# A decayed-attention, gated-product and slot-mixture kernel: the first sixteen items fetched further ahead, into six buffers

## The chip, the cores and the metric

The kernel runs on one core of one Trainium2 chip. The metric is the device time of one execution in microseconds (us), as a median of several runs. In a profile the engines are PE (TensorE: matmuls; PEld is its weight load), DVE (VectorE), ACT (ScalarE), POOL (GpSimd) and SP (SyncE, which here does nothing but issue transfers, in the order of its queue). "Span" is the time from the first to the last instruction.

## The reference, cut to what matters

```python
def _attn_ref(q, k, v, s):                      # B, H, S, D = 4, 8, 576, 64
    scores = scale * np.matmul(q, k.transpose(0, 1, 3, 2))
    cum = np.cumsum(np.maximum(s, 0.0), axis=-1)
    bias = -(cum[:, :, :, None] - cum[:, :, None, :])
    scores = np.where(causal, -1000000000.0, scores + np.minimum(bias, 0.0))
    attn = softmax(scores)                      # written out with max, exp, sum
    return np.matmul(attn, v)
...
def _moe_ref(x, w1, w2, w3, w_out):             # x: 2304 x 512
    a = x @ w1
    b = x @ w2
    return (a * b @ w3) @ w_out
...
def _moe2_ref(x, phi, w1, w2):                  # 8 experts, 4 slots each
    logits = x @ phi
    ...                                         # softmax over tokens, two expert layers, softmax over slots
    return c @ slot_out
```

All arrays are float32; the four matrices of `_moe_ref` arrive as 64-bit words (float64) and are converted on the chip.

## The kernel before, in words

Attention is cut into 40 items. Items 0 to 7 are heads 0 to 7 with the query tiles 0, 1, 2; items 8 to 15 are the same heads with the tiles 3, 4; items 16 to 39 are one head each with all five tiles. The first 16 items (`NF32`) multiply in float32: the item's tile `raw` holds queries and keys in 64 partitions, and four more partitions (64 to 67) get the decay rows of its head, so that one matmul gives score and decay. Items from 16 on are split into a rounded part `qa` and a rest `qb` by DVE and POOL.

An item passes through these steps. `att_fetch` issues the transfers of queries and keys; `att_prep` issues those of the decay rows and, for every second head, of the values `v` of two heads, and from item 16 on computes `qa` and `qb`. `att_scores` multiplies on PE (L334), adds the mask and takes the row minimum on DVE (L337) into the score buffer `sc`, and takes the exponential on ACT (L342). `att_norm` adds and inverts the row sums on DVE (L351, L352) and scales on POOL (L355). `att_transpose` turns the scores on PE (L370, and L384 for the diagonal blocks), into two PSUM buffers that ACT copies out (L372, L386). `att_pv` multiplies by the values of two heads (PE L110) and writes `x` (ACT L419, DVE L420). Then come the gated products `gl` (L432), which need `x` of four pairs of heads.

Beside this, the words of the matrices are fetched 512 KB at a time into three buffers (`fetch_words`, L178) and converted: ACT L186, DVE L189, L190, L193, then ACT L217 and POOL L218 for `w12`; ACT L186, L197, DVE L198, L201 for the others.

Buffers of a tile tag are a ring: the third `raw` waits until the first is read out. Before, `raw` has two buffers (`NRW`), `sc` three (`SCB`), and `qa` and `qb`, first used by item 16, two each (`QAB`). The program calls the steps in an order that `att_steps` and `weave` write out. SP's queue keeps that program order; the instructions on PE, DVE, ACT and POOL are put in order by the scheduler of the framework, so that a change of buffers or of waits also reorders those queues.

The lines around the fetch, as they stand before:

```python
            prep = [(0, lambda n=n: att_prep(n + 1, ap))] if n + 1 < N else []
            if n + 2 < N:
                prep += [(0, lambda n=n: att_fetch(n + 2, ap))]
```

Of the kernel before, what the change touches and what calls it, by code (L numbers as in the profile page):

```python
# [10 lines left out]
F32 = mybir.dt.float32  # L11
# [10 lines left out]
P = 128  # L22
B, H, S, D = 4, 8, 576, 64
# [24 lines left out]
def attn_glu_softmoe_kernel(  # L48
# [14 lines left out]
    nc = tc.nc  # L63
# [19 lines left out]

    NW, NRAW, NG4, NX, NE_ = 8, 3, 4, 6, 11
    NRW, SCB, PTB, QAB, VB = 2, 3, 2, 2, 2
    NF32, NDIR, ND = 16, 2, 1

    A1, CA, CB1, CB, GB1, GB, GC = 0.6, 8, 16, 26, 8, 16, 24

# [174 lines left out]
    hd = {}  # L264
    ITEMS = [(h, t) for t in ((0, 1, 2), (3, 4)) for h in range(H)] + [(h, (0, 1, 2, 3, 4)) for h in range(H, NH)]

    def att_fetch(n, ap):
        h, tiles = ITEMS[n]
        if h % 2 == 0:
            b, c = divmod(h // 2, H // 2)  # L270
            for blk, (_, nt, own) in enumerate(BLK):
                if own[0] in tiles:
                    x_t[b, blk, c] = xpl.tile([P, 2, nt], F32R, tag=f"x{blk}", name=f"x_{b}_{blk}_{c}", bufs=NX)
        q0, q1 = QT[tiles[0]][0], sum(QT[tiles[-1]])
        raw = ap.tile([P, 2, S], F32, tag="raw", name=f"raw_{n}", bufs=NRW)
        m = 64 if n < NF32 else P
        if q0:
            nc.sync.dma_start(raw[:m, 0, q0:q1], qk[h, 0, :m, q0:q1])
            nc.sync.dma_start(raw[:m, 1, :q1], qk[h, 1, :m, :q1])
        else:  # L280
            nc.sync.dma_start(raw[:m, :, :q1], qk[h, :, :m, :q1].rearrange("n p t -> p n t"))
        hd[n] = dict(raw=raw, q0=q0, q1=q1)

    def att_prep(n, ap):
        h, tiles = ITEMS[n]
        t = hd[n]
        raw, q0, q1 = t["raw"], t["q0"], t["q1"]
        if h % 2:
            vt = ap.tile([P, 9, 2, D], F32, tag="v", name=f"v_{n}", bufs=VB)
            nv = 2 * tiles[-1] + 1  # L290
            nc.sync.dma_start(vt[:, :nv], v[h // 2, :, :nv])
            t["v"] = hd[n - 1]["v"] = vt
        if n < NF32:
            rows = raw
        else:
# [22 lines left out]
    def att_scores(n, i, ap):  # L318
        t, tiles = hd[n], ITEMS[n][1]
        if i == tiles[0]:  # L320
            t["nmax"] = sm.tile([P, 6], F32, tag="nmax", name=f"nmax_{n}")
            t["rsum"] = rsum_t[n % 3]
            t["sc"] = ap.tile([P, 1600], F32, tag="sc", name=f"sc_{n}", bufs=SCB)
        nmax, rsum, mul = t["nmax"], t["rsum"], t["mul"]
        q0, r = QT[i]
        W = q0 + r
# [304 lines left out]
    def att_steps(ap):  # L631

        groups = [[] for _ in range(B + 1)]
        N = len(ITEMS)
        for n in range(N + 1):
            tiles = ITEMS[n][1] if n < N else ()
            old = [i for i in ITEMS[n - 1][1] if i] if 0 < n <= N else []
            sc = [(0.2 + 0.3 * i, lambda i=i, n=n: att_scores(n, i, ap)) for i in tiles]
            tr = [(0.2 + 0.3 * i, lambda i=i, n=n: att_transpose(n - 1, i, ap)) for i in old]
            norm = [(0, lambda n=n: att_norm(n - 1))] if 0 < n <= N else []  # L640
            prep = [(0, lambda n=n: att_prep(n + 1, ap))] if n + 1 < N else []
            if n + 2 < N:
                prep += [(0, lambda n=n: att_fetch(n + 2, ap))]
            blks = [k for k in range(2) if BLK[k][2][0] in ITEMS[n - 1][1]]
            pv = [(1.4, lambda n=n, k=k: att_pv(n - 2, k)) for k in blks] if n > 0 and n % 2 == 0 else []
            groups[min(B, max(0, (n - 1) // H))] += [
                *sc[:1], *norm, *sc[1:2], *prep, *sc[2:3], *tr[:1], *sc[3:4], *tr[1:2], *sc[4:], *tr[2:], *pv
            ]
        return groups
# [78 lines left out]
    with tc.tile_pool(name="att", bufs=1) as ap:  # L728
# [15 lines left out]
        hd["ap"] = ap  # L744
        att = att_steps(ap)
        decay_rows()
        att_prep(0, ap)
        for k in range(2, NRAW):
            fetch_words(k, ap)
        decay_store()  # L750

        def masks():

# [348 lines left out]
```

## Time and profile before

| | |
|---|---|
| median of 3 runs | 574.28 us (573.58 to 574.37) |
| span of the profiled execution | 569.3 us (4.98 below the median; the time of that execution itself is not listed apart) |
| PE busy | 519.9 us, 91% of the span |
| DVE, ACT, POOL busy | 316.7, 311.6, 194.7 us |
| transfers | 118.04 MB, 207 GB/s on average |

PE is busy almost everywhere except in the first tenth of the span and at its very end. A stretch in which PE is idle or runs at a lower clock is therefore where time can be found, and the other engines matter as far as PE waits for them.

### The profile page before, as it was taken

The page shows a single profiled execution, that of the slowest core. Times are in us where ns is not written, and L with a number is a line of the kernel's source. Part 1 is how long each engine was busy: PE and PEld are TensorE (multiplying, and loading weights), DVE is VectorE, ACT ScalarE, POOL GpSimd, SP SyncE. Part 2 cuts the span into 40 slices and gives each one's busy share as a digit, 9 for nine tenths or more (in the row PEclk, how much of TensorE's full clock was granted, in tenths as well). Part 3 has the DMA queues.
Part 4 walks back from the last instruction along what each step waited for, and adds up shares of the span by engine and source line. Part 5 has one row for each costly group of instructions (what it writes and reads, how often), then busy time and mean ns, then how long its engine had stood idle before and what let it go on. Part 6 is the DMA issues. An engine that isn't in the chain of part 4 may idle for free.

```text
span 569.3 us, 11835 instructions
## 1 busy us (share of the span) xinstructions
PE 519.9 (91%) x4288; PEld 434.2 (76%) x4288; DVE 316.7 (56%) x966; ACT 311.6 (55%) x845; POOL 194.7 (34%) x247
## 2 busy tenths in 40 slices
PE   1886999788899999999899999999999999999993
PEld 1664788666788897989899879898888999853452
DVE  6558676769987376656565757456640311243333
ACT  4577667666876665845576667456833321321222
POOL 5447531526678456252255444333210000000000
PEclk9998999979999999999999999999999999999997
DMA  6557557657763353536556554465351996689976
GB/s 197 188 164 229 183 180 252 238 170 237 224 218 116 119 165 108 169 95 205 176 155 189 170 185 139 156 200 163 123 212 48 368 411 233 238 295 423 421 296 235
DMA packets 38810, 118.04 MB, mean 207 GB/s; under 512 B 4224, under 2 KB 10560, under 8 KB 35296
## 3 DMA queue, kind: packets, MB, share of 16 engines
q1 hardware_dynamic: 36832, 113.74, 57.9%
q10 hardware_dynamic: 1920, 3.54, 2.5%
q8 instruction: 34, 0.56, 0.4%
q14 instruction: 24, 0.20, 0.1%
HBM read 102.11 MB, written 11.60 MB: 200 GB/s over the span
## 4 chain that ended last, share of the span: by engine, by line
PE 38%; DMA 5%; DVE 4%; ACT 2%; issue 1%; POOL 0%; SPq 0%; DVEq 0%; POOLq 0%; ACTq 0%
PE gl L432 17%; DMA raw_w<-in_w 4%; PE x_ps L110 3%; PE o_ps L1003 3%; PE h_ps L965 3%; PE gn_ps L602 2%; PE sc_ps L334 2%; PE pt_ps L370 2%; PE z_ps L110 1%; DVE w_w L198 1%; PE ptd_ps L384 1%; PE y_ps L889 1%; PE lg L110 1%; DVE sc L337 1%; DVE w_w L201 1%
## 5 line engine op out<-in xcount | busy, mean ns | idle before, releaser
L432 PE MATMUL gl<-x,w12t 128*128 128x320 f32 (+1 forms) x1536 | 241.0, 307 | 4.2 <-DVE nmax L337 2.4
L432 PEld LDWEIGHTS gl<-x,w12t 128*128 128x128 f32 x1536 | 215.4, 194 | 12.8 <-DVE nmax L337 4.3
L342 ACT ACTIVATE sc<-sc,nmax 128x64 f32<-128x64 f32 (+4 forms) x160 | 89.8, 563 | 40.4 <-DVE nmax L337 38.7
L355 POOL TENSOR_SCALAR sc<-sc,rinv 128x64 f32<-128x64 f32 (+4 forms) x160 | 91.0, 585 | 56.7 <-DVE rinv L352 45.8
L313 POOL TENSOR_TENSOR qa<-raw,qa 64x576 fp32r<-64x576 f32 x24 | 36.9, 1536 | 145.5 <-DVE qa L307 134.0
L337 DVE CUSTOM_DVE_ANT_0 sc<-sc_ps,mask 128x64 f32<-128x64 f32 (+4 forms) x160 | 65.3, 424 | 35.6 <-PE sc_ps L334 32.8
L372 ACT COPY pt<-pt_ps 128x128 f32<-128x128 f32 (+3 forms) x128 | 52.4, 422 | 27.8 <-PE pt_ps L370 18.1
L370 PE MATMUL pt_ps<-ident,sc 128*128 128x128 f32 x320 | 56.6, 288 | 5.4 <-POOL sc L355 4.3
L370 PEld LDWEIGHTS pt_ps<-ident,sc 128*128 128x128 f32 x320 | 39.5, 146 | 16.7 <-POOL sc L355 7.7
L334 PE MATMUL sc_ps<-qa 128*128 128x64 f32 (+1 forms) x144 | 46.2, 334 | 5.3 <-DVE nmax L337 2.3
L334 PE MATMUL sc_ps<-raw 68*128 68x288 f32 (+4 forms) x96 | 33.8, 495 | 17.8 <-DMA raw<-rows 13.3
L438 ACT COPY a<-gl 128x256 f32<-128x256 f32 (+1 forms) x64 | 25.4, 397 | 38.4 <-PE gl L432 34.8
L110 PE MATMUL x_ps<-pt,v 128*64 128x256 f32 (+1 forms) x384 | 45.8, 352 | 0.0
L334 PE MATMUL sc_ps<-qb 68*128 68x64 f32 (+1 forms) x144 | 43.7, 307 | 0.7 <-issue 0.7
L310 POOL TENSOR_TENSOR qb<-raw,qa 64x576 fp32r<-64x576 f32 x24 | 38.0, 1582 | 2.2 <-issue 0.5
L974 POOL MEMSET ht<- 128x1024 f32 x2 | 1.9, 954 | 107.3 <-DVE ew L878 98.4
L334 PEld LDWEIGHTS sc_ps<-raw 68*128 68x128 f32 x96 | 19.5, 241 | 23.4 <-issue 12.4
L110 PEld LDWEIGHTS x_ps<-pt,v 128*64 128x64 f32 x384 | 31.1, 139 | 6.9 <-issue 0.9
L186 ACT ACTIVATE w_w<-raw_w 128x512 f32<-128x512 f32 x32 | 21.6, 674 | 23.5 <-DMA raw_w<-in_w 22.4
L420 DVE TENSOR_TENSOR x<-x_ps,x 128x320 fp32r<-128x320 f32 (+1 forms) x32 | 14.0, 453 | 36.5 <-ACT x L419 36.5
L334 PEld LDWEIGHTS sc_ps<-qa 128*128 128x128 f32 x144 | 27.5, 191 | 8.7 <-DVE nmax L337 4.1
L605 ACT COPY gn<-gn_ps 128x512 f32<-128x512 f32 x40 | 22.7, 582 | 15.2 <-PE gn_ps L602 14.8
(180 smaller groups left out, 786.5 us busy)
## 6 DMA issues: line engine op xcount, KB each, us to landing
ew<-in_ew SPq DMA_DIRECT2D x27, 1024.0 KB
raw_w<-in_w SPq DMA_DIRECT2D x32, 512.0 KB
raw<-in_qk SPq DMA_DIRECT2D x24, 576.0 KB
v<-in_v SPq DMA_DIRECT2D x16, 576.0 KB
raw_w3t<-in_w3t SPq DMA_DIRECT2D x16, 512.0 KB
raw_wot<-in_wot SPq DMA_DIRECT2D x8, 512.0 KB
raw_wo<-in_wo SPq DMA_DIRECT2D x8, 512.0 KB
w_d<-w_w SPq DMA_DIRECT2D x8, 512.0 KB
```

The source lines that it names most:

```text
L110: mm = nc.tensor.matmul(out_, lhs, rhs, start=start, stop=stop)
L310: nc.gpsimd.tensor_tensor(out=qb[0:64, 1, :q1], in0=rk[0:64, :q1], in1=qa[0:64, 1, :q1].bitcast(F32), op=ALU.subtract)
L313: nc.gpsimd.tensor_tensor(out=qa[64:, 0, q0:q1], in0=rq[64:, q0:q1], in1=qa[64:, 0, q0:q1].bitcast(F32), op=ALU.subtract)
L334: nc.tensor.matmul(pp[:r, : z - a], x[:, 0, q0 : q0 + r], x[:, 1, a:z], start=x is mul[0], stop=x is mul[-1])
L337: nc.vector.tensor_tensor_reduce(out=sc[:r, a:z], in0=pp[:r, : z - a], in1=hd["mask"][:r, m0 : m0 + z - a], scale=-0.125, scalar=3.0e38 if ...
L342: nc.scalar.activation(out=sc[:r, :W], in_=sc[:r, :W], func=AF.Exp, bias=nmax[:r, i : i + 1], scale=-1.0, accum_out=rsum[:r, i, 0:1],)
L355: nc.gpsimd.tensor_scalar(out=sc, in0=sc, scalar1=rinv[:, i : i + 1], scalar2=1.0, op0=ALU.mult, op1=ALU.mult)
L370: nc.tensor.transpose(tp[:, j * P : (j + 1) * P], sc[:, j * P : (j + 1) * P], ident)
L372: t["turned", i] = nc.scalar.copy(out=pt[:, p0 : p0 + step * (i - 1) + 1 : step], in_=tp[:, : i * P].rearrange("p (j q) -> p j q", q=P))
L432: nc.tensor.matmul(acc[:, :nt], w12_t[fc][:, wi, n, kc], x_t[b, blk, kc][:, xi], start=k == 0, stop=k == 3 * KC - 1)
L438: nc.scalar.copy(out=a_sb[:, :nt], in_=acc[:, :nt])
L605: st["turned", blk, k, h] = nc.scalar.copy(out=gn[:r, 4 * h : 4 * h + 4].rearrange("p c f -> p (c f)"), in_=tp[:r])
```

## The change

Four things are done. The fetch of queries and keys of an item below 16 is issued four items ahead (before: two), and that of its decay rows three ahead (before: one). The tiles of these items use the tags `raw`, `qa` and `qb` in turn, two buffers each, six in all. The transfer of the values gets its own function and stays one item ahead. Of the items 0 to 7, an odd one uses the upper half of the score buffer of the even one before it. At the start, the decay rows of items 0 and 1 and the fetches of items 2 and 3 are issued before the loop, item 2's fetch ahead of the third block of words.

```diff
-    NF32, NDIR, ND = 16, 2, 1
+    NF32, NDIR, ND, FAR = 16, 2, 1, 3
...
-        raw = ap.tile([P, 2, S], F32, tag="raw", name=f"raw_{n}", bufs=NRW)
+        tag = ("raw", "qa", "qb")[n % 3] if n < NF32 else "raw"
+        raw = ap.tile([P, 2, S], F32, tag=tag, name=f"raw_{n}", bufs=NRW)
...
+    def att_values(n, ap):
+        h, tiles = ITEMS[n]
+        if h % 2:
+            vt = ap.tile([P, 9, 2, D], F32, tag="v", name=f"v_{n}", bufs=VB)
+            nv = 2 * tiles[-1] + 1
+            nc.sync.dma_start(vt[:, :nv], v[h // 2, :, :nv])
+            hd[n]["v"] = hd[n - 1]["v"] = vt
+
...
-            t["sc"] = ap.tile([P, 1600], F32, tag="sc", name=f"sc_{n}", bufs=SCB)
+            if n >= H or n % 2 == 0:
+                t["sc"] = ap.tile([P, 1600], F32, tag="sc", name=f"sc_{n}", bufs=SCB)
+            else:
+                t["sc"] = hd[n - 1]["sc"][:, 800:]
...
-            prep = [(0, lambda n=n: att_prep(n + 1, ap))] if n + 1 < N else []
-            if n + 2 < N:
-                prep += [(0, lambda n=n: att_fetch(n + 2, ap))]
+            prep = [(0, lambda n=n: att_values(n + 1, ap))] if n + 1 < N else []
+            d = FAR if n + FAR < NF32 else 1 if NF32 <= n + 1 < N else 0
+            if d:
+                prep += [(0, lambda m=n + d: att_prep(m, ap))]
+            d = FAR + 1 if n + FAR + 1 < NF32 else 2 if NF32 <= n + 2 < N else 0
+            if d:
+                prep += [(0, lambda m=n + d: att_fetch(m, ap))]
...
-        att_prep(0, ap)
+        for n in range(NDIR):
+            att_prep(n, ap)
+        att_fetch(2, ap)
         for k in range(2, NRAW):
             fetch_words(k, ap)
         decay_store()
+        for n in range(NDIR, FAR):
+            att_fetch(n + 1, ap)
+            att_prep(n, ap)
```

The change moves instructions on every engine. Three places show it. The number behind a tile's name is its item (or matrix block) and then a running number.

On SP near the start, before the change, from the third block of words (`raw_w12_1_0`) to the decay rows of item 2:

```order
L178 DMA raw_w12_1_0_153<-in_w12 128x512
L166 DMA rows_d_101<-rows_0_130 32x4x512
L166 DMA rows_d_101<-rows_1_131 32x4x512
L167 DMA rows_d_101<-rows_2_132 256x1x64
L291 DMA v_1_168<-in_v 128x640
L300 DMA raw_1_116<-rows_0_130 2x2x320
L300 DMA raw_1_116<-rows_1_131 2x2x320
L281 DMA raw_2_173<-in_qk 64x2x320
L178 DMA raw_w12_1_1_203<-in_w12 128x512
L302 DMA raw_2_173<-rows_d_101 4x2x320
```

The same place on SP after the change, from the second of item 1's two decay-row transfers to the fourth block of words:

```order
L304 DMA raw_1_116<-rows_1_131 2x2x320
L282 DMA raw_2_156<-in_qk 64x2x320
L178 DMA raw_w12_1_0_158<-in_w12 128x512
L166 DMA rows_d_101<-rows_0_130 32x4x512
L166 DMA rows_d_101<-rows_1_131 32x4x512
L167 DMA rows_d_101<-rows_2_132 256x1x64
L282 DMA raw_3_163<-in_qk 64x2x320
L306 DMA raw_2_156<-rows_d_101 4x2x320
L290 DMA v_1_176<-in_v 128x640
L306 DMA raw_3_163<-rows_d_101 4x2x320
L282 DMA raw_4_180<-in_qk 64x2x320
L178 DMA raw_w12_1_1_209<-in_w12 128x512
```

The decay rows of item 1 and the queries and keys of item 2 now stand ahead of the third block of words, and those of items 3 and 4 ahead of the fourth.

On PE around the transposes of item 0, before the change (`pt_ps` and `ptd_ps` are the two PSUM buffers in turn):

```order
L370 MATMUL pt_ps_0_1_214<-ident_86,sc_0_159 128x128
L370 MATMUL pt_ps_0_2_217<-ident_86,sc_0_159 128x128 x2
L334 MATMUL sc_ps_2_0_0_228<-raw_2_173 128x64
L334 MATMUL sc_ps_2_1_0_238<-raw_2_173 128x192
L334 MATMUL sc_ps_2_2_0_248<-raw_2_173 128x320
L384 MATMUL ptd_ps_0_221<-ident_86,sc_0_159 128x128 x3
```

The same place on PE after the change:

```order
L377 MATMUL pt_ps_0_1_220<-ident_86,sc_0_167 128x128
L377 MATMUL pt_ps_0_2_223<-ident_86,sc_0_167 128x128 x2
L391 MATMUL ptd_ps_0_227<-ident_86,sc_0_167 128x128 x3
L341 MATMUL sc_ps_2_0_0_234<-raw_2_156 128x64
L341 MATMUL sc_ps_2_1_0_244<-raw_2_156 128x192
L341 MATMUL sc_ps_2_2_0_254<-raw_2_156 128x320
```

The diagonal transposes of item 0 moved from behind item 2's scores to ahead of them.

On POOL around the split of item 16, before the change (L355 scales the scores of an item, L313 and L310 make the rests of `qa` and `qb`):

```order
L355 TENSOR_SCALAR sc_13_989<-sc_13_989,rinv_13_1057 128x576
L313 TENSOR_TENSOR qa_16_1238<-raw_16_1096,qa_16_1238 64x576
L310 TENSOR_TENSOR qb_16_1237<-raw_16_1096,qa_16_1238 64x576
L355 TENSOR_SCALAR sc_14_1052<-sc_14_1052,rinv_14_1196 128x448
L355 TENSOR_SCALAR sc_14_1052<-sc_14_1052,rinv_14_1196 128x576
```

The same place on POOL after the change:

```order
L362 TENSOR_SCALAR sc_13_965<-sc_13_965,rinv_13_1054 128x576
L362 TENSOR_SCALAR sc_14_1049<-sc_14_1049,rinv_14_1192 128x448
L362 TENSOR_SCALAR sc_14_1049<-sc_14_1049,rinv_14_1192 128x576
L317 TENSOR_TENSOR qa_16_1205<-raw_16_1092,qa_16_1205 64x576
L314 TENSOR_TENSOR qb_16_1204<-raw_16_1092,qa_16_1205 64x576
```

The scaling of item 14 moved ahead of the split of item 16; on DVE the reciprocal of item 14 likewise stands ahead of item 16's casts now. Elsewhere the scores of items 5 to 9 stand earlier on PE among the other work, and on DVE the write of `x` for the fourth pair of heads (L420) stands behind the conversion of block `w12_5_0`, where before it stood behind that of `w12_6_0`. Whole groups change places up to about item 18 and single instructions up to item 22; from there on the queues of PE, DVE, ACT and POOL are the same as before.

## Rows read from the trace of the kernel before

**Rows 1.** The page: busy us, share of the span and instructions of each engine.

```profile
PE 519.9 (91%) x4288; PEld 434.2 (76%) x4288; DVE 316.7 (56%) x966; ACT 311.6 (55%) x845; POOL 194.7 (34%) x247
```

**Rows 2.** Windows: length, busy us of PE, PEld, DVE, ACT, POOL, PEclk, DMA share, GB/s.

```profile
9.00:37.00 28.00, 21.44 (x82) 15.75 (x82) 16.44 (x62) 17.71 (x56) 14.30 (x21) 1.00 0.57 175
37.00:64.00 27.00, 21.01 (x138) 15.80 (x138) 21.51 (x60) 18.89 (x53) 16.16 (x19) 0.87 0.65 202
64.00:100.00 36.00, 34.99 (x238) 28.60 (x238) 23.35 (x63) 24.33 (x58) 10.70 (x13) 1.00 0.69 224
100.00:125.00 25.00, 19.03 (x127) 15.44 (x126) 17.61 (x40) 14.99 (x37) 10.65 (x8) 0.86 0.64 211
```

**Rows 3.** Waits of PE, 9 to 126 us: total, times, longest.

```profile
PE sc_ps L334 <- DMA raw<-rows: 13.3, 2, 9.6
...
PE sc_ps L334 <- DMA raw<-rows_d: 3.2, 4, 1.5
```

**Rows 4.** Timeline of PE, scores: start, us, and idle time before.

```profile
15.79 2.47 PE L334 MATMUL sc_ps<-raw 68*128 68x64 f32 x6 [3.71 <-DMA raw<-rows]
...
18.69 2.36 PE L334 MATMUL sc_ps<-raw 68*128 68x64 f32 x6
...
35.58 1.33 PE L334 MATMUL sc_ps<-raw 68*128 68x64 f32 x6 [0.43 <-issue]
```

**Rows 5.** Windows of 2 us (columns as in the windows above).

```profile
50.00:52.00 2.00, 0.33 (x1) 0.14 (x1) 1.97 (x5) 1.70 (x5) 2.00 (x4) 0.90 1.01 245
52.00:54.00 2.00, 1.17 (x2) 0.79 (x3) 1.92 (x4) 0.12 (x1) 1.29 (x1) 0.50 1.05 298
...
56.00:58.00 2.00, 2.00 (x10) 1.81 (x8) 2.00 (x7) 1.60 (x4) 0.71 (x1) 0.50 0.05 8
```

**Rows 6.** Timeline of SP near the start (the DMA queue's issues).

```profile
8.40 0.39 SPq L178 DMA_DIRECT2D raw_w<-in_w  x1
...
12.09 1.32 SPq L300 DMA_DIRECT2D raw<-rows  x2
13.51 0.69 SPq L281 DMA_DIRECT2D raw<-in_qk  x1
...
32.44 0.33 SPq L291 DMA_DIRECT2D v<-in_v  x1
```

**Rows 7.** Waits of SP, 9 to 60 us.

```profile
SPq L291 <- PE x_ps L110: 6.5, 2, 6.2
```

**Rows 8.** Timeline of DVE and ACT.

```profile
12.67 0.67 ACT L186 ACTIVATE w_w<-raw_w 128x512 f32<-128x512 f32 x1 [0.72 <-DMA raw_w<-in_w]
...
21.77 0.56 ACT L342 ACTIVATE sc<-sc,nmax 128x320 f32<-128x320 f32 x1
...
29.33 0.23 DVE L337 CUSTOM_DVE_ANT_0 sc<-sc_ps,mask 128x64 f32<-128x64 f32 x1 [0.99 <-PE ptd_ps L384]
...
30.86 0.55 ACT L342 ACTIVATE sc<-sc,nmax 128x320 f32<-128x320 f32 x1
...
38.96 0.43 ACT L419 CAST x<-x_ps 128x320 fp32r<-128x320 f32 x1
```

**Rows 9.** Groups of instructions by line, 9 to 56 us: busy us, mean ns of one.

```profile
L342 ACT ACTIVATE sc<-sc,nmax 128x64 f32<-128x64 f32 (+4 forms) x27 | 13.0, 480 | 4.0 <-DVE nmax L337 3.0 <-POOL sc L355 0.8
...
L193 DVE SCALAR_TENSOR_TENSOR w_w<-raw_w,w_w 128x512 uint32<-128x512 uint32 x10 | 8.5, 851 | 0.0
L190 DVE SCALAR_TENSOR_TENSOR w_w<-raw_w,w_w 128x512 int32<-128x512 int32 x9 | 6.4, 709 | 0.1
```

**Rows 10.** Timeline: the fourth `x`, and the split of item 16 on DVE, POOL and PE.

```profile
67.11 0.49 DVE L420 TENSOR_TENSOR x<-x_ps,x 128x320 fp32r<-128x320 f32 x1 [0.95 <-ACT x L419]
...
99.86 0.46 DVE L307 CAST qa<-raw 128x576 fp32r<-128x576 f32 x1 [1.89 <-DMA raw<-in_qk]
...
103.42 2.76 POOL L355 TENSOR_SCALAR sc<-sc,rinv 128x448 f32<-128x448 f32 x2
...
104.56 0.55 PE L370 MATMUL pt_ps<-ident,sc 128*128 128x128 f32 x3 [1.94 <-POOL sc L355]
```

More of the change, by code (lines that the diff above doesn't have):

```diff
@@ L287, in att_prep @@
         raw, q0, q1 = t["raw"], t["q0"], t["q1"]
[L288 to L292, printed above, removed]
         if n < NF32:
```

## The prediction

> **What bounds the kernel now.** I read the page first: PE is busy for 91% of the span [rows 1], so only stretches where it waits or runs slowly can give time back. The windows then show where these are. From 64 to 100 us PE is busy 34.99 of 36 us; from 9 to 37 it lacks 6.6 us, from 37 to 64 it lacks 6.0, from 100 to 125 again 6.0 [rows 2]. The change moves whole groups in the queues up to about item 18, whose work lies around the end of these windows, and single instructions up to item 22, so these three gaps are what it can reach. What is won there should reach the end whole: the later queues are as before, and the engines in them wait for each other, so that a shift is passed on. I count the single swaps behind item 18 at nothing, with a bound of 1 us to either side, about what one such order cost DVE at 29.33 (0.99) [rows 8].
>
> Next I read who ends PE's waits. Scores waited for decay rows 13.3 us in two waits, of which 9.6 are the start itself; that leaves 3.7. For decay rows out of memory they waited 3.2 us in four waits [rows 3]. So transfers hold PE for 6.9 us. Second comes the clock. Six score matmuls take 2.47 us at 15.79 and 1.33 at 35.58 [rows 4], and after a stretch in which PE was busy 0.33 of 2 us the granted clock is 0.50, the lower level of 1.2 GHz; it is still there at 56 to 58 with PE fully busy [rows 5]. A late transfer thus costs more than its wait. Third come the engines behind PE: from 37 to 64 us DVE is busy 21.51 of 27 us and ACT 18.89 [rows 2], so there they are nearly as full as PE, and a score that is computed earlier still has to pass them.
>
> **The change, step by step.** *The start gives little.* Item 1's scores stood idle for 3.71 us before 15.79 [rows 4]; their rows are now issued right behind item 0's, so they can start at 12.1. But the third block of words now stands on SP behind those rows (1.32) and item 2's queries (0.69), so it goes out at 10.4 and not at 8.40 [rows 6]. Before, ACT took it up at 12.67 after a wait for exactly this transfer [rows 8], which is 4.3 us after issue; now that makes 14.7. On ACT and DVE its conversion stands between the second and the third tile of item 1, and both engines keep their order. So: 14.7, ACT 0.67, a first DVE step and the third tile's minimum (about 0.5 each), its exponential about 0.75, which gives 17.1; then ACT's copies of item 0's transposes, whose PSUM the diagonal transposes need, and these now stand ahead of item 2's scores. That puts item 2's scores at about 18.4, and they were at 18.69 [rows 4]. The fourth block of words moves back likewise, behind items 3 and 4, by about 2.3 us, and stands on ACT ahead of item 2's last exponential: I get 21.9 for that, and it was 21.77 [rows 8]. Up to here I count **0 us**; the bounds are a loss of 1 (the words land later still) and a gain of 3.7 (the words land early enough).
>
> *Items 4 to 7.* Before, DVE stood 0.99 us at 29.33 for the score buffer, until item 1's diagonal transposes were done, and item 4's last exponential came at 30.86 [rows 8]. With two items in a buffer this wait is gone, and the rows of items 3 and 4 are there. PE goes through item 3, item 1's transposes and item 4 without a stop from 20.8 to 26.7, at the slow rate of rows 4, and the last exponential comes at about 28.3: 2.5 us earlier. After that items 5, 6 and 7 follow before the second pair's `x`, which comes at about 41.8 by the same reckoning, where it was 38.96 [rows 8]: 2.85 later, but with two more items through their exponentials. Two items are six exponentials of 0.48 us [rows 9] plus their read-outs, about 3.4 us of ACT. ACT works at 18.89 of 27 [rows 2], so this is 4.8 us of the time before; net 2.0. By DVE, at 21.51 of 27, the two items are worth some 3.2 us; net 0.4. Taken between: **1.2 us**.
>
> *From the second to the fourth `x`.* Up to the fourth `x` DVE now converts two and a half blocks fewer. A block costs DVE 0.85 and 0.71 [rows 9] and a third step of about 0.5, so 2.1 us, and 5.2 for them all. In the stretch before, DVE was full (1.97 and 1.92 of 2) just while PE stood nearly idle [rows 5], so a part of this comes off the path: at DVE's rate of 0.80 up to 6.5 us, at worst nothing, if PE's own work fills the place. The half clock from about 52 to 59 is worth another 3.5 us (seven busy us at half rate), but it lies in the same place and I don't count it twice. I take half of the 6.5, **3.2 us**, because PE, which was full at half clock from 54 on, becomes the next to be late. So the fourth `x`, at 67.11 before [rows 10], comes at about 62.7. The conversions left over fall into the stretch to 100 us, in which DVE idles 12.65 of 36 us while PE idles 1 [rows 2]: they cost nothing there. If that cover were gone, they would cost their 5.2 us.
>
> *Item 16.* Before, DVE stood 1.89 us for item 16's queries; POOL split item 16 first and scaled item 14 only at 103.42, and PE waited 1.94 us for that [rows 10]. Now the scaling comes first on POOL and its reciprocal first on DVE, and the fetch of item 16 waits for item 12's buffer and not for item 14's. I count the **1.9 us** of PE. The split is then later by the 2.76 us of that scaling at most; POOL was free from 106 to 112, so this is hidden. Bounds: 0 (another wait takes its place) and 4 (the clock of 0.86 in this stretch [rows 2] improves too).
>
> *The values and the copies.* The transfers are as many as before and of the same size. Splitting the values from the rows and the new tags cost no instruction. The wait of SP that remains is that for the values of items 4 and 5, which need the product of the first pair: 6.2 us until 32.44 before [rows 6, 7]. Queued behind it are now item 7's rows, item 8's queries and the seventh block of words, where before it was item 5's rows. I get that product's end at about 33.5 and item 7's rows 2.5 us later, just when PE comes to them: 0, bounds 0 and minus 2.
>
> Sum: 0 + 1.2 + 3.2 + 1.9 = 6.3 us. The span of 569.3 becomes 563.0. The profiled execution's own time isn't listed; the median lies 4.98 above the span, and with the same distance the time is **568.0 us**.
>
> **A rule weighed.** At 52 to 54 us the DMA share is 1.05 [rows 5], and there lies PE's longest wait for rows out of memory, 1.5 us [rows 3], before item 9. The Trainium skill, "DMA: Bandwidth & Descriptors", section "Issuing engines are not separate DMA queues", says that all transfers run on the same 16 DMA engines and interleave; by that rule an earlier fetch makes bytes no fewer, and what is pulled ahead pushes the words back. This trace agrees in that place, and for the whole stretch (share 0.65, rows 2) it leaves room. By the row for the stretch the sum stays; by the rule applied to the burst alone, the wait at item 9 stays and the sum is 3.4 lower. That is the third rival.
>
> **The rivals.** *All waits go.* If the words land early enough, the change gives PE's 6.9 us of transfer waits [rows 3], half of the slow clock at the start is gone with them, the 3.5 us of half clock, and 1.9 at item 16: some 13 us, 561. For it speaks that ACT and DVE idle 10 and 11.6 us between 9 and 37 [rows 2]; against it the order on ACT, where words stand between tiles. Chance 0.20.
>
> *The work of DVE and ACT sets the pace.* Then only item 16 is won and the rest returns as waits for L337 and L342: 572 to 574. For it speaks 21.51 of 27; against it that two and a half blocks leave the stretch. Chance 0.12, a third of it below the 0.2% line.
>
> *The burst stays.* The transfers of values and words still come in a heap behind SP's wait, item 9's rows are late again and the clock falls again: 571.4. Chance 0.13.
>
> *Slower: SP's wait for the values grows.* Behind it stand item 7's rows and three transfers on which PE's next work hangs. If the first pair's product ends after about 36 us, the rows land after 38.5, PE idles for longer than two us with nothing else in its queue, and the clock falls as in rows 5: some 2 to 4 us of wait, 3.5 of half clock, against the 1.2 and 1.9 won elsewhere, and the conversions come on top when DVE has no idle time left: 575.5 to 578. Against it speaks that item 5's rows stood behind the same wait before. Chance 0.11.
>
> **How the numbers follow.** The forecast has 0.44 (565 to 571). Faster by over 0.2% (about what a measurement of this kernel can tell from no change, 1.15 us) takes the forecast, the first and the third rival and a third of the second: 0.80. The same: 0.09. Slower: 0.11. The range is 561.5 to 575.0: it leaves out half of the first rival and most of the last, 2 in 10 together. The forecast's own range is 565 to 571.
>
> **What the next profile would show.** Right: item 1's scores at about 12 with no wait for rows, but item 2's still at about 18; no wait of DVE for the diagonal transposes at item 4; the fourth `x` on DVE at 61 to 64; no granted 0.50 near 52 to 58; PE full from there to item 16, and no wait of PE for POOL's scaling of item 14. Wrong: an ACT wait for words at 14 to 15 that is absent (then more is won), a PE idle time of over 2 us before item 7 or item 9 (then less), or PE waiting for `w12` blocks between 64 and 100.

## The result and the profile after

The changed kernel takes 566.29 us (median of 4 runs, 563.34 to 568.55) beside 574.33 us (573.58 to 575.59) for the kernel before: ratio 0.9849, 95% interval 0.9814 to 0.9883. The forecast was 568.0 us. The medians differ by 8.0 us, where the sum of the prediction was 6.3. A second comparison, in another group of runs (after_again, below), gave 0.9805 (0.9755 to 0.9855), a difference of 10.3 us. The profiled execution took 565.44 us. Lines of the code are 7 higher than before from `att_scores` on (L334 is L341 now).

The page of the changed kernel:

```profile
span 563.6 us, 11844 instructions
...
PE 520.0 (92%) x4288; PEld 433.9 (77%) x4288; DVE 316.2 (56%) x966; ACT 310.0 (55%) x845; POOL 196.7 (35%) x247
```

PE's busy time is that of [rows 1], so in these two executions the span shrank by the idle time of PE alone (569.3 less 563.6). The windows, as in [rows 2], show where:

```profile
9.00:37.00 28.00, 24.02 (x92) 18.15 (x92) 18.83 (x75) 18.58 (x64) 17.40 (x24) 1.00 0.63 187
37.00:64.00 27.00, 22.51 (x142) 17.06 (x141) 18.14 (x45) 16.01 (x46) 12.02 (x14) 0.87 0.76 223
64.00:100.00 36.00, 35.93 (x226) 29.71 (x227) 29.29 (x71) 25.91 (x60) 20.65 (x18) 0.95 0.67 217
100.00:125.00 25.00, 23.85 (x202) 19.65 (x201) 22.61 (x52) 19.24 (x49) 8.30 (x6) 1.00 0.78 257
```

Length less busy time of PE is 4.0, 4.5, 0.1 and 1.2 us, where it was 6.6, 6.0, 1.0 and 6.0: 9.8 us less idle time up to 125 us, more than the 5.7 that the span keeps. The waits of PE, 9 to 126 us, as in [rows 3]:

```profile
PE sc_ps L341 <- DMA raw<-rows: 9.6, 1, 9.6
PE ptd_ps L391 <- ACT pt L379: 3.8, 4, 1.6
PE pt_ps L377 <- ACT pt L379: 1.6, 3, 0.7
PE sc_ps L341 <- DVE w_w L193: 1.2, 1, 1.2
PE pt_ps L377 <- POOL sc L362: 1.0, 1, 1.0
...
PE sc_ps L341 <- DMA raw<-rows_d: 0.4, 1, 0.4
```

Only the start itself (9.6) still waits for rows. Of the 3.7 us before item 1 and the 3.2 us for rows out of memory 0.4 are left. The longest waits left are for ACT, whose copies stand behind words that came late. PE's timeline (second group: item 0's diagonal transposes, third: items 2 and 3's scores, fifth: item 9's scores), against [rows 4]:

```profile
15.21 1.19 PE L377 MATMUL pt_ps<-ident,sc 128*128 128x128 f32 x3 [0.99 <-POOL sc L362]
17.88 0.90 PE L391 MATMUL ptd_ps<-ident,sc 128*128 128x128 f32 x3 [1.48 <-ACT pt L379]
19.13 3.54 PE L341 MATMUL sc_ps<-raw 68*128 68x64 f32 x10 [0.35 <-DMA raw<-rows_d]
...
34.31 0.55 PE L391 MATMUL ptd_ps<-ident,sc 128*128 128x128 f32 x3 [0.37 <-ACT pt L379]
...
43.25 3.62 PE L341 MATMUL sc_ps<-raw 68*128 68x448 f32 x6 [1.17 <-DVE w_w L193]
```

Three diagonal transposes take 0.85 to 0.90 us at the lower clock (the 17.88 row) and 0.49 to 0.55 at the higher (the 34.31 row). They serve below to see when the clock first rises. The timeline of ACT and DVE, against [rows 8, 10]:

```profile
15.45 0.67 ACT L186 ACTIVATE w_w<-raw_w 128x512 f32<-128x512 f32 x1 [1.19 <-DMA raw_w<-in_w]
...
23.53 0.66 ACT L186 ACTIVATE w_w<-raw_w 128x512 f32<-128x512 f32 x1 [2.01 <-DMA raw_w<-in_w]
24.10 0.55 ACT L349 ACTIVATE sc<-sc,nmax 128x320 f32<-128x320 f32 x1
...
29.17 0.55 ACT L349 ACTIVATE sc<-sc,nmax 128x320 f32<-128x320 f32 x1
...
60.83 0.66 ACT L186 ACTIVATE w_w<-raw_w 128x512 f32<-128x512 f32 x1 [3.87 <-DMA raw_w<-in_w]
...
63.31 0.48 DVE L427 TENSOR_TENSOR x<-x_ps,x 128x320 fp32r<-128x320 f32 x1
```

The waits for words at 15.45, 23.53 and 60.83 are the price of the rows' earlier issue. Item 4's last exponential is at 29.17 (30.86 before), the fourth `x` at 63.31 (67.11).

What was won is not all kept. DVE's writes of `x` for items 14/15, 16/17 and 18/19 and for the last pair, before:

```profile
137.88 0.41 DVE L420 TENSOR_TENSOR x<-x_ps,x 128x256 fp32r<-128x256 f32 x1
166.09 0.80 DVE L420 TENSOR_TENSOR x<-x_ps,x 128x320 fp32r<-128x320 f32 x2
183.30 0.82 DVE L420 TENSOR_TENSOR x<-x_ps,x 128x320 fp32r<-128x320 f32 x2 [2.70 <-ACT x L419]
...
441.39 0.82 DVE L420 TENSOR_TENSOR x<-x_ps,x 128x320 fp32r<-128x320 f32 x2 [12.18 <-ACT x L419]
```

and after:

```profile
125.53 0.42 DVE L427 TENSOR_TENSOR x<-x_ps,x 128x256 fp32r<-128x256 f32 x1
153.44 0.82 DVE L427 TENSOR_TENSOR x<-x_ps,x 128x320 fp32r<-128x320 f32 x2
176.34 0.82 DVE L427 TENSOR_TENSOR x<-x_ps,x 128x320 fp32r<-128x320 f32 x2 [2.67 <-ACT x L426]
...
436.17 0.82 DVE L427 TENSOR_TENSOR x<-x_ps,x 128x320 fp32r<-128x320 f32 x2 [12.18 <-ACT x L426]
```

The lead is 12.35 and 12.65 us, then 6.96, and 5.22 at the last pair. (Up to about item 18 the order on PE differs, so the first two leads hold some order too.) Between 153 and 176 us lies a heap of transfers. SP's issues after 150 us, and the windows (columns as above):

```profile
151.04 1.67 SPq L178 DMA_DIRECT2D raw_w3t<-in_w3t  x2
152.76 0.42 SPq L290 DMA_DIRECT2D v<-in_v  x1
153.28 0.28 SPq L306 DMA_DIRECT2D qb<-rows_d  x1
153.66 0.38 SPq L282 DMA_DIRECT2D raw<-in_qk  x1
155.54 0.34 SPq L178 DMA_DIRECT2D raw_w3t<-in_w3t  x1
155.96 0.52 SPq L306 DMA_DIRECT2D qb<-rows_d  x1
156.53 0.38 SPq L282 DMA_DIRECT2D raw<-in_qk  x1
```

```profile
155.00:160.00 5.00, 1.99 (x18) 1.75 (x16) 2.32 (x5) 1.65 (x4) 1.09 (x1) 0.94 0.93 313
160.00:165.00 5.00, 3.79 (x27) 3.15 (x28) 3.31 (x7) 4.29 (x13) 1.81 (x2) 0.50 0.67 244
```

Three blocks of words of 512 KB, values of 576 and twice queries and keys of 576 are 3.3 MB, at 313 GB/s some 10 us from 151.04 on. PE resumed in that time with a score that reads decay rows out of `qb`:

```profile
161.21 0.39 PE L341 MATMUL sc_ps<-qb 68*128 68x64 f32 x1 [4.21 <-issue]
```

The row names no releaser. The trace holds it elsewhere: the transfer of these rows, issued at 153.28, makes its last semaphore update at 161.12, just ahead of this score. ACT waited 3.35 us for words until 159.21. After this pause the granted clock was at 0.50, the lower of the two levels (1.2 of 2.4 GHz). The pair after_again and before_again has the same loss at the same place: there the lead falls from 15.54 to 9.37 us between the same two writes, and is 10.65 at the last.

### The profile page after: what moved, and what is told of

Its sections match the earlier page's. It is cut to its first block, busy times and chain, and to the rows that moved or that the text cites. A ratio compares the mean times of both kernels' runs of the same rounds, so it can differ in the third digit from the quotient of the medians.

```text
span 563.6 us, 11844 instructions
## 1 busy us (share of the span) xinstructions
PE 520.0 (92%) x4288; PEld 433.9 (77%) x4288; DVE 316.2 (56%) x966; ACT 310.0 (55%) x845; POOL 196.7 (35%) x247
## 5 line engine op out<-in xcount | busy, mean ns | idle before, releaser
L439 PE MATMUL gl<-x,w12t 128*128 128x320 f32 (+1 forms) x1536 | 238.3, 304 | 1.3 <-DVE nmax L344 0.7
L439 PEld LDWEIGHTS gl<-x,w12t 128*128 128x128 f32 x1536 | 212.2, 191 | 10.0 <-issue 4.3
L362 POOL TENSOR_SCALAR sc<-sc,rinv 128x64 f32<-128x64 f32 (+4 forms) x160 | 92.4, 594 | 53.9 <-DVE rinv L359 39.2
L341 PE MATMUL sc_ps<-qa 128*128 128x64 f32 (+1 forms) x144 | 46.6, 336 | 6.0 <-DVE nmax L344 2.5
L377 PEld LDWEIGHTS pt_ps<-ident,sc 128*128 128x128 f32 x320 | 38.8, 145 | 17.3 <-issue 10.0
L341 PE MATMUL sc_ps<-qb 68*128 68x64 f32 (+1 forms) x144 | 44.2, 310 | 4.2 <-issue 4.2
L110 PE MATMUL x_ps<-pt,v 128*64 128x256 f32 (+1 forms) x384 | 47.5, 353 | 0.0
L341 PE MATMUL sc_ps<-raw 68*128 68x288 f32 (+4 forms) x96 | 35.5, 514 | 11.1 <-DMA raw<-rows 9.6
L341 PEld LDWEIGHTS sc_ps<-qa 128*128 128x128 f32 x144 | 27.7, 192 | 9.1 <-DVE nmax L344 3.5
L341 PEld LDWEIGHTS sc_ps<-raw 68*128 68x128 f32 x96 | 21.2, 259 | 16.3 <-issue 12.1
L341 PEld LDWEIGHTS sc_ps<-qb 68*128 68x128 f32 x144 | 28.0, 194 | 4.6 <-issue 4.4
```

Of the source, the lines that this page charges most:

```text
L110: mm = nc.tensor.matmul(out_, lhs, rhs, start=start, stop=stop)
L341: nc.tensor.matmul(pp[:r, : z - a], x[:, 0, q0 : q0 + r], x[:, 1, a:z], start=x is mul[0], stop=x is mul[-1])
L362: nc.gpsimd.tensor_scalar(out=sc, in0=sc, scalar1=rinv[:, i : i + 1], scalar2=1.0, op0=ALU.mult, op1=ALU.mult)
L377: nc.tensor.transpose(tp[:, j * P : (j + 1) * P], sc[:, j * P : (j + 1) * P], ident)
L439: nc.tensor.matmul(acc[:, :nt], w12_t[fc][:, wi, n, kc], x_t[b, blk, kc][:, xi], start=k == 0, stop=k == 3 * KC - 1)
```

## The experiments

Each ratio is to the kernel before in the same group of runs. "PE busy" is that of the whole span, from each page. "Idle" is PE's idle time and "matmuls" what it issued from 9 to 125 us, from the windows of [rows 2]. "First high" is the first group of three diagonal transposes that takes 0.55 us or less; such groups stand up to 12 us apart, so it dates the rise no finer than that. "Low later" is (1 less granted clock) times twice the length, over the windows 37:64, 64:100, 100:125, 125:150, 150:175, 175:200 and 200:300. The granted clock reads 1.00 until the first change that a trace records. Where that change, a rise, comes behind 37 us (at 42.61 in shared_only, 45.43 in far_only, 37.08 in near_six, 58.86 in words_first), the time from 37 us to it is added.

| kernel | median us | ratio (95%) | span | PE busy | idle | matmuls | first high | low later |
|---|---|---|---|---|---|---|---|---|
| before (first profile) | 574.33 | | 569.3 | 519.9 | 19.5 | 585 | 34.61 | 21.5 |
| before_again | 576.22 | 1.0026 (0.9983 to 1.0068) | 573.3 | 524.2 | 17.3 | 606 | 34.21 | 30.5 |
| after (first profile) | 566.29 | 0.9849 (0.9814 to 0.9883) | 563.6 | 520.0 | 9.7 | 662 | 34.31 | 17.6 |
| after_again | 564.88 | 0.9805 (0.9755 to 0.9855) | 562.2 | 520.4 | 10.0 | 698 | 34.59 | 13.0 |
| shared_only | 578.02 | 1.0030 (0.9993 to 1.0066) | 577.4 | 527.8 | 17.3 | 561 | 43.57 | 39.1 |
| far_only | 576.17 | 1.0002 (0.9975 to 1.0029) | 575.8 | 532.2 | 10.6 | 578 | 47.38 | 39.6 |
| near_six | 580.74 | 1.0085 (1.0053 to 1.0117) | 579.0 | 527.6 | 16.5 | 583 | 37.18 | 38.6 |
| words_first | 581.59 | 1.0125 (1.0075 to 1.0174) | 578.1 | 532.9 | 7.0 | 604 | 60.70 | 42.0 |
| values_later | 571.73 | 0.9935 (0.9899 to 0.9972) | 569.5 | 526.4 | 12.8 | 587 | 37.84 | 26.8 |
| before_filled | 573.61 | 0.9938 (0.9901 to 0.9974) | 572.2 | 524.8 | 19.2 | 583 | 32.51 | 27.5 |
| after_filled | 565.49 | 0.9803 (0.9756 to 0.9851) | 565.8 | 523.2 | 11.1 | 687 | 34.55 | 14.0 |
| after_kept_busy | 569.35 | 0.9890 (0.9845 to 0.9936) | 566.8 | 528.9 | 9.8 | | 17.24, 0.60 | 22.3 |
| far_kept_busy | 562.11 | 0.9766 (0.9709 to 0.9822) | 563.8 | 527.7 | 7.5 | | 23.35 | 14.0 |
| far_kept_busy_27 | 563.60 | 0.9789 (0.9749 to 0.9830) | 561.4 | 523.4 | 10.3 | | 26.85 | 6.0 |

(after_kept_busy's first group spans a rise. In the last three the clock is also up for a while before the first such group, and their matmuls and busy times count the added transposes, as the busy times of the two filled kernels do.)

Span less PE busy is PE's idle time over the whole execution, and it falls into two groups. Where the fetch is near (before, before_again, shared_only, near_six) it is 49.1 to 51.4 us; where it is far, with no transposes added (after, after_again, far_only, words_first, values_later), 41.8 to 45.2. PE's busy time, for the same 4288 matmuls, goes from 519.9 to 532.9 us. It is longest where "first high" and "low later" are largest. So in every order seen the far fetch comes with some 4 to 10 us less idle time, and whether the kernel gets shorter by that depends on what the order does to the clock. A PE at the lower clock waits less by itself, but at about equal busy time shared_only and near_six idle for 49.6 and 51.4 us and values_later for 43.1. This rests on one trace of each kernel, and on two of the kernel before and of the changed one.

**The two parts.** shared_only puts the sharing of score buffers into the kernel before; far_only takes it out of the changed one:

```diff
-            t["sc"] = ap.tile([P, 1600], F32, tag="sc", name=f"sc_{n}", bufs=SCB)
+            if n >= H or n % 2 == 0:
+                t["sc"] = ap.tile([P, 1600], F32, tag="sc", name=f"sc_{n}", bufs=SCB)
+            else:
+                t["sc"] = hd[n - 1]["sc"][:, 800:]
```

> The kernel before, with only the score buffer of the first eight items shared by two; fetches as before. My theory: the wait of DVE for the score buffer near 29 us goes, but PE's waits for rows (3.2 us), the half clock near 50 to 56 and the idle time of PE around item 16 (POOL still splits item 16 ahead of scaling item 14) stay, so only the term of 1.2 us comes: 572 to 574 us. Rival (score buffers are what held the pipeline): most of the gain comes with it, 566 to 569 us.

> The changed kernel with a score buffer for each item, as before; fetches 3 to 4 items ahead in six buffers. My theory: rows no longer wait, POOL scales item 14 ahead of the split of item 16, and only the 1.2 us of the shared buffer are missing: 566.5 to 569 us, with a wait of DVE for ptd of some 1 us near 29 us. Rival (the far fetch is worth nothing while scores have no buffer): 572 to 575 us.

Both come out at the time before, so far_only's rival held in time; but the table shows that it held for another reason. far_only has almost the short idle time of the whole change (10.6 us; over the whole span 43.6 in both), and loses it by the clock: PE is busy for 12.2 us more with the same matmuls. PE's line on its page, its window, two rows of PE and one of DVE:

```profile
PE 532.2 (92%) x4288; PEld 442.3 (77%) x4288; DVE 311.9 (54%) x966; ACT 311.1 (54%) x845; POOL 194.8 (34%) x247
```

```profile
37.00:64.00 27.00, 22.17 (x103) 15.56 (x102) 13.93 (x50) 15.07 (x46) 11.60 (x16) 0.85 0.67 201
```

```profile
30.20 1.01 PE L338 MATMUL sc_ps<-raw 68*128 68x192 f32 x2 [1.64 <-DVE nmax L341]
...
47.38 0.55 PE L388 MATMUL ptd_ps<-ident,sc 128*128 128x128 f32 x3 [1.24 <-ACT pt L376]
```

```profile
36.12 0.23 DVE L341 CUSTOM_DVE_ANT_0 sc<-sc_ps,mask 128x64 f32<-128x64 f32 x1 [1.81 <-PE ptd_ps L388]
```

PE is as busy as in the changed kernel (22.51) and does 103 matmuls in place of 142: the first rise of the clock comes some 12 us later (45.43 against 33.15 by the change that each trace records first). At the first pair's product, where the changed kernel's PE does not pause, this one waits 1.64 us for DVE's read-out, and DVE itself had stood 1.12 us for ACT's first step on a block of words. That this wait is what delays the rise was not tested. The wait for the score buffer that I expected near 29 us is not there; a wait for diagonal transposes of 1.81 us stands at 36.12, and PE pauses for 0.22 us beside it. Taking the shared buffers out leaves PE's idle time as it was, and so does putting them in alone (49.6 us in shared_only, 49.4 before): by these traces the sharing saves no idle time, and what it adds to the change it adds through the order.

**The distance.** near_six is the changed kernel with the old distances:

```diff
-    NF32, NDIR, ND, FAR = 16, 2, 1, 3
+    NF32, NDIR, ND, FAR = 16, 2, 1, 1
```

> The changed kernel with FAR = 1: six buffers and shared score buffers, but rows one item ahead and queries and keys two ahead, as before. On POOL item 16 is split ahead of the scaling of item 14 again. My theory (distance counts): PE's waits for rows out of memory come back, 2 to 3 us between 15 and 60 us, the idle time of PE behind item 16 too, 571 to 574 us. Rival (buffers alone count, because they decouple the fetches from the items before): 566 to 568 us.

The distance counts: PE's idle time is 16.5 us again, 2.3 of it for rows out of memory. It is 0.85% slower than before, which neither theory had; PE's idle time over the whole span, 51.4 us, is the longest of all, and its "low later", 38.6 us, is near those of shared_only and far_only.

**The words at the start.** words_first issues the third block of words ahead of item 2:

```diff
-        att_fetch(2, ap)
         for k in range(2, NRAW):
             fetch_words(k, ap)
+        att_fetch(2, ap)
         decay_store()
```

> The changed kernel with the third block of words issued ahead of item 2's queries and keys, behind item 1's rows. My theory (late words eat what the start wins): ACT takes the third block 0.7 us earlier, at 14.7 instead of 15.45, item 2's scores come at 18.4 to 18.8, and the time is 565 to 566.5 us, hardly to be told from the change as it is. Rival (the start does not reach the end, because a later heap of transfers sets it): item 2 earlier, the end the same, 566 to 567 us with the same spread of single runs (563 to 569).

Both were wrong. Up to 125 us it has the shortest idle time of the four (7.0 us), and it is the slowest:

```profile
37.00:64.00 27.00, 25.44 (x115) 18.06 (x115) 15.51 (x44) 15.27 (x43) 11.71 (x15) 1.00 0.53 165
```

```profile
35.27 0.90 PE L391 MATMUL ptd_ps<-ident,sc 128*128 128x128 f32 x3 [0.32 <-ACT pt L379]
...
60.70 0.49 PE L391 MATMUL ptd_ps<-ident,sc 128*128 128x128 f32 x3
```

PE is busier than in the changed kernel (25.44 against 22.51) and does a fifth fewer matmuls (115 against 142): the clock first rises later than in any other run. The column of the granted clock says 1.00 there, which cannot be so; it shows 1.00 until the first change of the clock that the trace holds, here the rise at 58.86 (after_filled, below, shows it too). Over the whole span PE is busy for 532.9 us, 12.9 more than in the changed kernel, and idles for 45.2.

**The controls.**

> The kernel before, once more with a profile, on the chip of this group. The four kernels of the first group ran beside a kernel before of 576.3 us (570.9 to 580.6), and in their traces a 128x128 transpose still took 421 ns at 40 to 56 us, where the first profiles of both kernels show 272 ns from about 36 us on. My theory (the moment at which TensorE's clock rises differs from run to run and from chip to chip, and with it the time): the transposes of this run fall to 272 ns at another time than 36 us when its time is over 576, near 36 us when it is 574 or less. Rival (transfers are slower on such a chip): the rise is at 36 us in any case, and PE's waits for rows and words between 9 and 126 us add up to over 2 us more than the 3.2 and 4.0 of the first profile.

> The changed kernel once more, in five rounds, as the control for all other runs. If the change is worth 1.5% whatever the chip: ratio 0.981 to 0.989. Rival (the four runs had a lucky clock, and the parts that gave 1.000 to 1.003 in the first group say what the whole is worth): ratio 0.993 to 1.005, and the profile shows transposes of 421 ns until 40 us or later.

before_again has its first rise where the first profile had it, so my theory of a chance moment fell: two runs each put it at 34.61 and 34.21 before and at 34.31 and 34.59 after, and the first changes that the traces record lie at 34.53 and 34.15, and at 33.15 and 33.81. For a given order the moment repeats; in the other orders, with one trace each, it lies elsewhere. The later falls do not repeat: "low later" is 21.5 and 30.5 us in the two runs before. The change keeps its gain in this group. The waits of PE from 96 to 126 us in before_again:

```profile
PE wot_ps L110 <- DVE u_sb L258: 2.5, 1, 2.5
...
PE pt_ps L370 <- POOL sc L355: 0.6, 1, 0.6
```

The wait for POOL's scaling, 1.94 us in [rows 10], is 0.6 here; what both runs before share in this stretch is the wait for `u_sb` and the half clock (0.86 in the window 100:125). Both runs after have neither.

**A filled start.** 16 transposes of the identity, read by nothing, stand ahead of the first scores, in both kernels; no other instruction moves:

```diff
         make_identity(nc, ident)
+        fill = psum("tp", "fill")
+        for _ in range(16):
+            nc.tensor.transpose(fill[:, :P], ident, ident)
```

> The kernel before with 16 transposes of the identity on PE ahead of the first scores (their results are read by nothing); the order of all other instructions on all five engines is the same. PE idles there until 9.6 us anyway. My theory (the late rise of the clock costs time, and it comes late because PE has idled): the clock is up at the first scores, six score matmuls of an item take 1.3 instead of 2.5 us there, and the time falls by 2 to 6 us against the kernel before, with less spread. Rival (PE waits for others at the start, or the clock falls again in the first gap): within 0.3% of the kernel before.

> The changed kernel with the same 16 transposes ahead of the first scores; all other orders as in the changed kernel. My theory (what the change gives is hidden or shown by the clock's rise): 2 to 6 us below the changed kernel of this group, less spread, and the difference to before_filled shows what the change is worth with the clock out of the way: I expect 3 to 7 us. Rival: no difference to the changed kernel, within 0.3%.

The rival held for after_filled (0.9803 beside 0.9805); before_filled does not part the two theories: its median is 1.6 us (0.3%) below the kernel before, its ratio 0.6%. The two filled kernels differ by 8.1 us, more than the 3 to 7 that I expected, but the clock was not out of the way: in both it is low again after the start. The trace of after_filled has the clock's fall, so its first window reads otherwise than the changed kernel's with the same work (24.02, x92, 1.00):

```profile
9.00:37.00 28.00, 23.99 (x88) 17.90 (x89) 18.32 (x75) 18.80 (x64) 16.99 (x24) 0.57 0.63 186
```

**PE kept busy.** 20 such transposes at the start, and two behind each score tile and each transposed tile of items 0 to 5, in the changed kernel and in far_only:

```diff
+            if n < 6:
+                fill(pp, 2)
...
+        if n < 6:
+            fill(tp, 2)
```

> The changed kernel with 20 transposes of the identity on PE ahead of the first scores, and two behind every read-in of a score tile and every transpose of a score tile of the first six items, into columns of the same PSUM tiles that nothing reads. My theory (in all ten traces so far the span goes with the time at half clock between 9.6 and 300 us, about 0.48 us for each us: 37 to 41 us at a span of 562 to 566, 65 to 70 us at 576 to 579; and the clock is low because PE pauses): the clock is up from 6 to 10 us on instead of from 33, and the kernel comes to 557 to 563 us. Rival (the added work takes PE's place in an order that waits for PE, or the clock falls in spite of it): 565 to 573 us.

> The same added transposes in the kernel far_only (fetches 3 to 4 items ahead, a score buffer for each item), which took 576.2 us with the clock first up at 45.4 us. My theory (far_only loses to the changed kernel by the clock and hardly by its waits): within 1% of after_kept_busy, 558 to 568 us. Rival (the score buffer's wait itself is what it loses by): 572 to 578 us.

far_only becomes 2.4% faster, some 14 us, with more work on PE: 0.9766 in place of 1.0002. With the 12.2 us of busy time above, this speaks for the clock, and not the waits, as what cost it the gain of the far fetch. A caution is that the added work also reorders PE, and that the theory failed for after_kept_busy: its clock rises early as well and is low again at 36.79 us, and it takes some 0.4 to 0.9% more than the changed kernel (0.9890 beside 0.9849 and 0.9805), with 60 transposes of 0.11 to 0.21 us added behind the start. The relation of span to low clock that its expectation states does not hold there.

far_kept_busy_27 has 27 transposes at the start in place of 20:

> far_kept_busy with 27 transposes ahead of the first scores in place of 20; the orders of the engines differ in four rows each on PE, DVE and ACT. In far_kept_busy the 20 ended at 6.52 us, PE idled 3.10 us for the first rows, and the granted clock fell near 9.3 us until 19.6 us. With 27 the pause shrinks to about 1.6 us. My theory (the pause lets the clock fall, and the low clock at the start costs): the clock stays up past 9.6 us, item 0's and 1's scores take half the time, and the kernel comes to 557 to 561 us. Rival (up to 20 us DVE, ACT, POOL and the rows set the pace, or the clock falls in the shorter pause too): 561 to 564 us, as far_kept_busy.

The mechanism was right for the first scores and its worth nothing (the median lies in the rival's range). PE in far_kept_busy, and in far_kept_busy_27:

```profile
2.45 4.07 PE L268 MATMUL fill<-ident 128*128 128x128 f32 x20 [2.45 <-POOL ident masks.py:199]
9.62 0.66 PE L342 MATMUL sc_ps<-raw 68*128 68x64 f32 x2 [3.10 <-DMA raw<-rows]
```

```profile
2.45 4.74 PE L268 MATMUL fill<-ident 128*128 128x128 f32 x27 [2.45 <-POOL ident masks.py:199]
9.22 0.41 PE L342 MATMUL sc_ps<-raw 68*128 68x64 f32 x2 [2.02 <-DMA raw<-rows]
...
14.93 0.33 PE L380 MATMUL pt_ps<-ident,sc 128*128 128x128 f32 x1 [1.58 <-POOL sc L365]
```

With the shorter pause the first scores take 0.41 us in place of 0.66, and then PE waits 1.58 us for POOL: there others set the pace, and a faster PE only waits.

**The values later.**

```diff
-            prep = [(0, lambda n=n: att_values(n + 1, ap))] if n + 1 < N else []
+            prep = [(0, lambda m=n if n < NF32 else n + 1: att_values(m, ap))] if n + 1 < N else []
```

> The changed kernel with the values of the first 16 items issued one item later, so that SP waits less for the product of the first pair; POOL splits item 16 ahead of scaling item 14 again. By the step of the prediction that counted SP's wait at nothing: SP's two waits of 6.1 and 6.7 us shrink to under 3 each, and the time stays within 1 us of the changed kernel, 564 to 567; the reversed order on POOL alone would cost up to 1.9. Rival (orders matter through the clock alone): a time that follows the first rise of the clock, 572 or more if it comes after 42 us, 561 to 566 if it comes at 33 or 34.

Missed: SP's waits for the pairs' products grew instead of shrinking, to 17.5 us, the longest 12.0:

```profile
SPq L290 <- PE x_ps L110: 17.5, 3, 12.0
```

POOL's order is the one before, and PE does not wait for POOL between 96 and 126 us. PE's idle time over the whole span is 43.1 us, that of the changed kernel (43.6), and its busy time 6.4 us longer, so in this trace the loss lies in the rate of PE's matmuls and not in more waiting for SP or POOL. Of the rival's cases, the rise at 37.84 and the time of 571.7 lie between the two.

## Why the prediction was right, and where its steps were not

The time lay inside the stated range (566.3 against 568.0), and the places of the gain were the right ones. That the numbers come so near is partly luck, in two ways. First, at the writes of `x` for items 14 to 17 the lead was 12.4 to 12.7 us, about twice the sum of 6.3, and a loss that was not foreseen took half of it. (Up to about item 18 a part of such a lead is order.) Second, the spans differ by 5.7 us, but the medians by 8.0 and 10.3. In every execution of which both are listed, the time lies 1.7 to 1.9 us above the span (565.44 and 563.6 here), so the profiled execution of the kernel before took about 571 us (an estimate), 3 less than its median. The prediction's distance of 4.98 was mostly this, and with 1.8 the same sum would have given 564.8 us.

- *The start, 0*: nearly as told. Item 1's scores come with no wait, the third block of words is taken up at 15.45 (predicted 14.7), and item 2's scores are at 19.13 (18.4; before 18.69). Item 2's last exponential is at 24.10, 2.2 us later than predicted, because the fourth block made ACT wait 2.01 us: it was issued at 19.41, 5.1 us later than before and not 2.3, after SP had itself waited 1.9 us for decay rows in memory.
- *Items 4 to 7, 1.2*: DVE's wait for the score buffer at item 4 is gone (the first profile has one of 1.34 us at 47.98, in the half-clock stretch, after_again none), item 4's last exponential is at 29.17 (28.3), the second pair's `x` on ACT at 40.32 (41.8). PE's idle time from 9 to 37 us is 2.6 us shorter. That the wait itself is worth this was not shown: shared_only alone gives nothing, and far_only, without the shared buffers, idles as little as the whole change.
- *Second to fourth `x`, 3.2*: the fourth `x` is at 63.31 (62.7), so this term and the one before came to 3.8 us together, where the sum had 4.4. The half clock of 52 to 58 us did not vanish; in the profiled run it fell earlier, behind PE's 1.17 us before item 9, and the score row of 3.62 us at 43.25 runs in it. In after_again the window 37:64 has a granted clock of 1.00, so this part differs between runs.
- *Item 16, 1.9*: the term that failed in size. PE's idle time from 100 to 125 us fell by 4.8 us (3.3 from before_again to after_again), and the granted clock rose from 0.86 to 1.00. The wait named was not the cause that repeats: POOL's scaling cost 0.6 us in before_again, and the wait for `u_sb` and the clock were the rest. far_only, whose PE is busy for 25.00 of 25 us there, and near_six, with 21.83 and a wait of 2.6 us for `u_sb`, show that the far fetch brings it.
- *SP's wait for the values, 0*: right. SP waits 6.1 us, goes on at 32.28, and item 7's scores at 35.16 do not wait for rows. A second wait of SP, of 6.7 us until 51.52, was not in the sum.
- *Not foreseen*: that the lead shrinks from 12.65 to 6.96 us between 153 and 176 us. In after_again it shrinks at the same place, from 15.54 to 9.37. I had taken what is won by 125 us to reach the end whole. The kernel runs into a heap of transfers with PE idle for 4.2 us and the clock low after it; the rival "the burst stays" had this mechanism, but at item 9 (its 3.4 us are not worked out from the rows it names).

The rule weighed in the prediction (the Trainium skill, "DMA: Bandwidth & Descriptors", "Issuing engines are not separate DMA queues") agrees with the later place: at a DMA share of 0.93 four partitions of rows issued at 153.28 held PE until about 161.

What stays open is why the first rise comes at 34 us in one order and at 60 in another. In words_first PE has no pause above 0.32 us between its 18.25 and 46 us and its transposes stay slow. The traces show that it goes with the order, and not which property of the order does it. What the traces do show is that the far fetch takes away idle time of PE in each order tried. That the measured time gains by it is a property of this order: PE's busy time is the same before and after (519.9 and 520.0 us), while far_only and three small edits to the change (near_six, words_first, values_later) lengthened it by 6 to 13 us and gave the gain back in part or whole.

## What to carry to other kernels

Where a scheduler orders the engines, the parts of a change need not add: test the whole and the parts beside the kernel before, and split the span into PE's busy and idle time, since a PE at the lower clock looks just as busy and the busy time of the same matmuls then grows. A fetch further ahead moves the transfers, it doesn't make them fewer: look for the next place where they come in a heap. A faster start is worth what the engines behind PE leave of it.

## What was not expected of the hardware

- 28 us of nearly uninterrupted small float32 matmuls in words_first (18 to 46 us) left the clock at its lower level, while 27 transposes of the identity in a row, begun at 2.45 us, raised it before they ended: they took 4.74 us, and at the rate of before_filled and after_filled (16 in 3.68) would have taken about 6 (an estimate).
- The 20 transposes at the start of after_kept_busy and of far_kept_busy are the same work, begun at 2.46 and 2.45 us, and took 4.53 us in the one and 4.07 in the other. So the moment of a rise can differ where PE's work up to it does not.
- The granted clock reads 1.00 in a trace until its first recorded change, also where the matmul rates are those of the lower level (words_first up to 58.86 us). Durations of one shape (0.85 against 0.49 us here) are the safer reading.
- The Trainium skill, "TensorE: Matmul & The Clock Gate", "Part 1: The HAM clock gate", says that the moment at which the clock rises differs by about 0.5 us either way from run to run. This case's traces agree in size: the changes first recorded lie 0.4 us apart in the two runs before (34.53 and 34.15) and 0.7 us in the two after (33.15 and 33.81). Between orders of the same work it moved by up to 26 us (58.86 in words_first).
